# Attention with a learned distance bias, and a routed mixture of experts: the 64-row last tile of a batch regrouped from four units into two, with the planner's choices for the bias blocks and its ranks changed

## The chip, the cores and the metric

The kernel runs on one core of a Trainium2 chip. The metric is device time in microseconds (us) of one execution, the median of three runs: 261.92 us before the change (261.89 to 262.06).

## What is computed

Two batches of 8 heads, 576 positions and head size 64 go through attention; its rows, 1152 tokens of 512, go through a top-1 mixture of 8 experts with 288 places each. All arrays are float32.

```python
scores = scale * np.matmul(q, k.transpose(0, 1, 3, 2))
psi_rel = np.log1p(np.abs(rel))                    # rel = i - j
psi_i = np.log1p(np.maximum(pos[:, None], 1.0))
h = np.maximum((psi_rel / psi_i)[..., None] @ w1 + b1, 0.0)   # 32 hidden
scores = scores + (h @ w2).transpose(2, 0, 1)[None]           # a bias for each head, i, j
attn = softmax(scores)
x = np.matmul(attn, v)                             # to [1152, 512]
# each token: the expert with the largest gate logit, the first 288 tokens of an expert in order
out = gate * (relu(x_e @ w1_e) @ w2_e)             # 0 for tokens without a place
```

## The kernel before, in words

**Attention.** A batch's 576 rows are five tiles of rows: t = 0 to 3 hold 128 rows, t = 4 holds 64. The work runs over `units` (L507): the tiles of batch 0 in the order 4, 3, 2, 1, 0, then of batch 1 in the order 0 to 4, and in each tile four pairs of heads, 40 units in all. For a unit the planner has these tasks:

- S (`scores`, L181): the scores. In a 128-row tile, the two heads of a pair lie on the two halves of the array's rows, so four matmuls of 64 x 128 weights and 288 columns fill two PSUM buffers `s` (L195). In the 64-row tile, q is stored with zeros between the heads, so that two matmuls of the full array (L203) give both heads of the pair in one buffer: one head in partitions 0 to 63, the other in 64 to 127.
- L (`least`, L206): adds the bias and takes the row minimum of the negated scores (one VectorE instruction of 128 x 576 at L212; two for a unit of a 128-row tile, one for one of the 64-row tile). X (`expo`): the exponential on ScalarE (L219), with row sums.
- R and T (`transp_rem`, `transp`): transposes of the exponentials on TensorE, the last 64 positions (L266 in the 64-row tile) and the others (L241 there; `flips` at L227 in the other tiles); C: copies out of PSUM by ScalarE or VectorE (L250, L252, L273).
- V (`attn_v`, L275): values times transposed exponentials, the two heads on the two halves of the array's columns (L289; in the 64-row tile L292 with 64 columns, and L295 on two quadrants).

R, T, C and V of a unit follow two units (`LAG`) behind its S.

**The bias.** It depends on the rows alone, so both batches use it. 36 blocks of 16 rows each (`blocks`: tile 4's four blocks first, then those of tiles 3, 2, 1, 0) are made in this way: H, four instructions of the hidden layer (`hidden`, each a quarter c of the rows; GpSimd L122, ScalarE L124, VectorE L126); M, eight TensorE instructions on four column strips of the array (L141); E, a scaling out of PSUM by VectorE or ScalarE (L154, L156); D, a store to DRAM (L162). B loads a tile's bias back, skewed (L175, L178), once all its blocks are stored.

**Experts.** Routing constants and picks are small VectorE work. Expert weights come by 512 KB loads issued by GpSimd (L686), are split into two parts (L668, L670, L673) and used in three matmuls for each product (L723, L764, L792, L828). Most of the buffers for the second and third expert's weights take the place of attention's, so a task `late` lets them begin behind the last V.

**The order of work.** Every task has engines to choose from with a cost on each, tasks it comes after, buffers it takes, and a rank. `place_tasks` (L951) simulates the engines' queues with those costs and issues the tasks in the order it finds: of the tasks that can start within 0.3 us of the earliest, the one of least rank, on the engine that ends it first. `shift` adds a number to the rank of a kind of task. Before the planner starts, constants, the first K tiles and the first q are loaded. The order of each engine's queue is thus fixed when the program is built. The sync queue (SP) issues all stores and loads but the expert weights, indirect gathers and scatters, in order; a wait there holds all that stands behind.

## Time and profile before

| | |
|---|---|
| median of three runs | 261.92 us |
| the profiled execution | 260.9 us, its span 259.1 us |
| TensorE matmuls busy | 238.8 us, 92% of the span |
| VectorE, ScalarE, GpSimd busy | 194.0, 180.9, 106.9 us |
| moved by DMA | 58.63 MB, 226 GB/s over the span |

A busy TensorE is one with a matmul in flight; matmuls overlap, so their costs are best read from one start to the next. In the traces PE is TensorE, PEld its weight loads, DVE VectorE, ACT ScalarE, POOL GpSimd, SP the sync engine; a "q" behind a name is the engine's instruction queue. Tiles have the program's names: `s`, `tt`, `pt`, `av` are PSUM buffers, `ed` the scores and exponentials, `bt` the loaded bias, `bd` the bias in DRAM, `bo` a block of it ahead of its store, `hid` the hidden layer, `vt` the values.

### The profile page before, as it was taken

The numbers are of one execution on the slowest core, as the hardware profiler recorded it, in microseconds if no ns is written. First come the engines' busy times: TensorE is split into PE (matmuls) and PEld (weight loads), VectorE is DVE, ScalarE is ACT, GpSimd is POOL, SyncE is SP. The second block draws the span as 40 slices with busy tenths as digits, with TensorE's granted clock in tenths as the row PEclk, the third lists the DMA queues.
The fourth block names the chain that finished last, engine by engine and source line by source line (L and its number), as shares of the span: only waits on it lengthen the run. The fifth ranks groups of instructions, "written<-read, shape, count | busy, mean of one in ns | idle before, by whom it ended". The sixth has DMA issues, their size and how long they took to land.

```text
span 259.1 us, 7407 instructions
## 1 busy us (share of the span) xinstructions
PE 238.8 (92%) x2820; PEld 186.0 (72%) x2820; DVE 194.0 (75%) x551; ACT 180.9 (70%) x405; POOL 106.9 (41%) x112
## 2 busy tenths in 40 slices
PE   1997988999999999999999999999999999999950
PEld 0642544767755888888888877878898999999830
DVE  3898978999785756568989989588955799985200
ACT  4998998999998878787888778745202498832410
POOL 2999999999970200000123222001105948000410
PEclk9999999999999999999999999999999999999995
DMA  5589999989897862398689999800223799700210
GB/s 162 189 314 214 394 367 336 337 250 395 263 367 299 283 238 63 108 325 299 184 274 375 293 249 357 320 0 3 81 83 122 273 401 411 307 0 4 61 48 3
DMA packets 26620, 58.63 MB, mean 226 GB/s; under 512 B 3573, under 2 KB 4341, under 8 KB 26577
## 3 DMA queue, kind: packets, MB, share of 16 engines
q1 hardware_dynamic: 22224, 43.02, 49.6%
q0 software_dynamic: 4352, 15.06, 16.0%
q8 instruction: 24, 0.39, 0.6%
q14 instruction: 20, 0.16, 0.2%
HBM read 41.36 MB, written 16.99 MB: 225 GB/s over the span
## 4 chain that ended last, share of the span: by engine, by line
PE 69%; DMA 11%; issue 6%; DVE 5%; ACT 3%; POOL 2%; POOLq 0%; SPq 0%; DVEq 0%
PE s L195 11%; PE av L289 11%; PE tt L227 5%; PE s L764 5%; PE pt L723 5%; DMA bd<-bo 5%; PE tt L141 3%; PE pt L141 3%; DMA raw<-in_w_dram 3%; PE tt L764 3%; PE pt L764 3%; DMA bt<-bd 2%; PE s L203 2%; PE s L141 2%; PE tt L723 2%
## 5 line engine op out<-in xcount | busy, mean ns | idle before, releaser
L122 POOL TENSOR_SCALAR hid<-c_u,nbv 128x384 f32<-128x384 f32 (+17 forms) x48 | 68.7, 1447 | 2.2 <-PE tt L141 1.3
L212 DVE CUSTOM_DVE_ANT_0 ed<-s,bt 128x576 f32<-128x576 f32 x72 | 51.9, 754 | 18.4 <-PE s L227 12.0
L219 ACT ACTIVATE ed<-ed,mn 128x576 f32<-128x576 f32 x72 | 55.9, 785 | 2.1 <-DVE kept L584 1.3
L250 ACT COPY at<-tt 128x512 f32<-128x512 f32 x68 | 37.6, 590 | 17.9 <-PE tt L227 14.0
L195 PE MATMUL s<-kraw,q 64*128 64x288 f32 x256 | 40.8, 426 | 0.9 <-DVE rt L273 0.8
L289 PE MATMUL av<-at,vt 128*64 128x128 f32 x512 | 35.1, 279 | 0.0
L289 PEld LDWEIGHTS av<-at,vt 128*64 128x64 f32 x512 | 27.4, 136 | 6.0 <-issue 4.9
L195 PEld LDWEIGHTS s<-kraw,q 64*128 64x128 f32 x256 | 24.1, 186 | 9.5 <-issue 3.7
L126 DVE TENSOR_SCALAR hid<-c_u,c_v 128x464 f32<-128x464 f32 (+17 forms) x52 | 29.2, 609 | 0.1
L673 DVE TENSOR_TENSOR wl<-raw,wh 128x1024 fp32r<-128x1024 f32 x24 | 28.8, 1214 | 0.3 <-ACT wh L668 0.3
L124 ACT ACTIVATE hid<-c_u,c_v 128x448 f32<-128x448 f32 (+16 forms) x44 | 26.9, 668 | 2.9 <-DVE c_v L528 2.9
L434 POOL TENSOR_SCALAR tokv<-s 128x5 bf16<-128x5 f32 (+2 forms) x3 | 0.6, 206 | 67.8 <-DVE s L428 51.9
L686 POOL DMA_DIRECT2D raw<-in_w_dram x24 | 13.3, 560 | 27.7 <-DVE wl L673 15.7
L227 PE MATMUL tt<-c_ident,ed 64*128 64x64 f32 x512 | 22.6, 223 | 0.0
L227 PEld LDWEIGHTS tt<-c_ident,ed 64*128 64x128 f32 x512 | 19.6, 139 | 2.5 <-issue 0.5
L141 PE MATMUL pt<-hid,c_w2bd 128*32 128x496 f32 (+11 forms) x144 | 17.4, 513 | 1.8 <-ACT bo L156 1.0
L141 PE MATMUL tt<-hid,c_w2bd 128*32 128x512 f32 (+11 forms) x160 | 18.0, 471 | 0.1
L668 ACT CAST wh<-raw 128x1024 fp32r<-128x1024 f32 x16 | 16.8, 1049 | 0.5 <-DMA raw<-in_w_dram 0.4
L156 ACT ACTIVATE bo<-pt,corr,c_rv 128x192 f32<-128x192 f32 (+25 forms) x26 | 14.1, 595 | 0.9 <-PE pt L141 0.6
L493 POOL DMA_INDIRECT xe<-xd,sli x7 | 8.7, 1248 | 14.5 <-DVE hl L730 8.2
L219 ACT ACTIVATION_READ_ACCUMULATOR ed<-ed,mn 128x1 f32 x72 | 14.7, 204 | 0.0
L748 POOL DMA_INDIRECT out_dram<-y,sli x7 | 8.2, 1164 | 15.3 <-ACT sh L842 8.9
(272 smaller groups left out, 511.9 us busy)
## 6 DMA issues: line engine op xcount, KB each, us to landing
bt<-bd SPq DMA_DIRECT2D x28, 576.0 KB, 5.7
raw<-in_w_dram POOLq DMA_DIRECT2D x24, 512.0 KB, 7.0
bd<-bo SPq DMA_DIRECT2D x36, 295.5 KB, 5.8
vt<-in_v_dram SPq DMA_DIRECT2D x8, 320.0 KB, 5.2
kraw<-in_k_dram SPq DMA_DIRECT2D x8, 288.0 KB, 4.3
bt<-bd SPq DMA_DIRECT2D x8, 288.0 KB, 6.5
out_dram<-y SPq DMA_DIRECT2D x3, 768.0 KB, 12.5
q<-in_q_dram SPq DMA_DIRECT2D x8, 256.0 KB, 5.8
```

The lines of the kernel that those rows point to most:

```text
L122: nc.gpsimd.tensor_scalar(hid[:, :m], wu[:, :m], nbv[:, w:w + 1], None, op0=ALU.max)
L124: nc.scalar.activation(hid[:, :m], wu[:, :m], AF.Relu, bias=bvw[:, w:w + 1])
L126: nc.vector.tensor_scalar(hid[:, :m], wu[:, :m], bvw[:, w:w + 1], 0.0, op0=ALU.add, op1=ALU.max)
L141: nc.tensor.matmul(ps[32 * c:32 * c + 32, lo:hi], lhsT=w2bd, rhs=hids[n, c][:, lo:hi], start=True, stop=True, tile_position=(0, 32 * c))
L195: nc.tensor.matmul(ps[i][:, r, :HALF], lhsT=q[p, hp], rhs=k[p, r * HALF:(r + 1) * HALF], start=True, stop=True, tile_position=(64 * i, 0))
L212: nc.vector.tensor_tensor_reduce(out=ed.rearrange("p (r j) -> p r j", r=2), in0=ps[:, :, :HALF], in1=bias.rearrange("p (r j) -> p r j", r= ...
L219: nc.scalar.activation(ed, ed, AF.Exp, scale=-1.0, bias=mns.pop((n, i)), accum_out=total)
L227: nc.tensor.transpose(out[r][:w], ed[p, o:o + w], ident[p, p], tile_position=(64 * r, 0))
L250: nc.scalar.copy(o, v)
L289: nc.tensor.matmul(av[p, hp], lhsT=vt[:, j, i], rhs=at[:, 4 * i + j] if j < 4 else rt, start=(j == 0), stop=(j == 4), tile_position=(0, r))
L673: (nc.vector if eng == "d" else nc.gpsimd).tensor_tensor(lo, raw, hi.bitcast(F32), op=ALU.subtract)
L764: nc.tensor.matmul(py[:, :cap], lhsT=w, rhs=hx, start=(f + i == 0), stop=(f == 7 and i == 2))
```

## The change

- The 64-row tile of a batch has two units of two pairs of heads each instead of four units of one pair, 36 units in all. q of this tile is stored without zeros. Scores are eight matmuls of 64 x 64 weights on the four quadrants of the array (row half: head of the pair, column half: the pair), into two `s` buffers. L, X, R, T and C are then those of a 128-row tile, and V is two pairs' worth of matmuls with 64 columns; both pairs' K must be there for a unit, so the second K tile is loaded earlier.
- H of the first eight blocks may go to VectorE or ScalarE only (GpSimd was a choice for c = 3 of blocks 0 to 3, the only one for c = 3 and one of three for c = 2 of the others); for the other blocks c = 2 goes to ScalarE or GpSimd. Costs of H are new numbers, with another one for VectorE while GpSimd is at work.
- Loads of V of batch 0, the gate weights and the routing constants wait for no task; `v` has 8 buffers (4 before), `q` has 2 (3 before).
- The `shift` table has new numbers throughout, and new kinds: S, L, X, R, T, V and C by pairs of tiles, H, M, E, D by tile.

The core of the diff:

```diff
-    qp = keep.enter_context(tc.tile_pool(name="qp", bufs=3))
-    vp = keep.enter_context(tc.tile_pool(name="vp", bufs=4))
+    qp = keep.enter_context(tc.tile_pool(name="qp", bufs=2))
+    vp = keep.enter_context(tc.tile_pool(name="vp", bufs=8))
...
     def scores(n):
 
         b, t, hp = units[n]
-        if t < 4:
-            sc = [big.tile([128, 2, 512], F32, name="s") for _ in range(2)]
+        ps = [big.tile([128, 2, 512], F32, name="s") for _ in range(2)]
...
-        q, k = qs[b, t], raws[b, hp]
-        if t < 4:
-            ps = sc
-            for r in range(2):
+        q = qs[b, t]
+        for r in range(2):
+            for c, u in enumerate(pairs(n)):
+                o, w = (0, 128) if t < 4 else (64 * c, 64)
                 for i in range(2):
                     p = slice(64 * i, 64 * i + 64)
-                    nc.tensor.matmul(ps[i][:, r, :HALF], lhsT=q[p, hp], rhs=k[p, r * HALF:(r + 1) * HALF],
-                                     start=True, stop=True, tile_position=(64 * i, 0))
...
-        ps = big.tile([128, 2, 512], F32, name="s")
-        free[n] = [ps[:, r] for r in range(2)]
-        for r in range(2):
-            nc.tensor.matmul(ps[:, r, :HALF], lhsT=q[:, hp], rhs=k[:, r * HALF:(r + 1) * HALF], start=True, stop=True)
-        sx[n] = [(ps, ed[:, 0], sums_t[b, t][:, hp:hp + 1])]
+                    nc.tensor.matmul(ps[i][o:o + w, r, :HALF], lhsT=q[p, u, :w], rhs=raws[b, u][p, r * HALF:(r + 1) * HALF],
+                                     start=True, stop=True, tile_position=(64 * i, o))
+        free[n] = [z[:, 1] for z in ps]
...
     def attn_v(n):
...
+        for c, u in enumerate(pairs(n)):
+            o, w = (0, 128) if t < 4 else (64 * c, 64)
+            for j in range(5):
+                for i in range(2):
+                    r = 64 * i
+                    nc.tensor.matmul(av[r:r + 64, u, :w], lhsT=vs[b, u][:, j, i],
+                                     rhs=(at[:, 4 * i + j] if j < 4 else rt)[:, o:o + w],
                                      start=(j == 0), stop=(j == 4), tile_position=(0, r))
...
-    units = [(0, t, hp) for t in (4, 3, 2, 1, 0) for hp in range(4)] + \
-            [(1, t, hp) for t in (0, 1, 2, 3, 4) for hp in range(4)]
+    units = [(b, t, z) for b, t in order for z in range(4 if t < 4 else 2)]
...
     dma_q(*order[0])
+    dma_k(0, 1)
     ident = load_const("ident", [128, 128])
-    for hp in range(1, 4):
+    for hp in range(2, 4):
         dma_k(0, hp)
...
+        def cost(us, e, at):
+
+            return us["dp"] if e == "d" and "dp" in us and free_at["p"] > at else us[e]
...
-            engines = "p" if c == 3 and n >= 4 else "dap" if c == 2 and n >= 4 or c == 3 else "da"
-            task(("H", n, c), engines, {"d": 0.12 + m * 1.1e-3, "a": 0.2 + m * 0.83e-3, "p": m * 3.4e-3},
+            engines = "da" if n < 8 else ("da", "da", "ap", "p")[c]
+            task(("H", n, c), engines, {"d": 0.2 + m * 0.52e-3, "dp": 0.37 + m * 0.62e-3, "a": 0.2 + m * 0.83e-3, "p": 0.36 + m * 2.35e-3},
...
-            task(("VL", b, hp), "s", 0.45, (lambda b=b, hp=hp: dma_v(b, hp)), after=[slot(17) if b else slot(hp - 1) or then("B", 0, 4, 1)],
-                 rank=20.0 * b + hp - 1, takes=[("v", users)], kb=273)
-    task("wg", "s", 0.45, lambda: nc.sync.dma_start(out=wgt, in_=ins["wg"]), after=[slot(1)], rank=4.0, kb=32)
-    task("route", "s", 2.7, route_const, after=[slot(6)], rank=12.0, kb=300)
+            task(("VL", b, hp), "s", 0.45, (lambda b=b, hp=hp: dma_v(b, hp)), after=[slot(p1 - 3) if b else None],
+                 rank=p1 * b + hp - 1, takes=[("v", users)], kb=273)
+    task("wg", "s", 0.45, lambda: nc.sync.dma_start(out=wgt, in_=ins["wg"]), rank=4.0, kb=32)
+    task("route", "s", 2.7, route_const, rank=12.0, kb=300)
...
-        task(("V", n), "e", 1.15 if full else 0.79, (lambda n=n: attn_v(n)),
+        task(("V", n), "e", 1.15 if full else 1.6, (lambda n=n: attn_v(n)),
...
-    qr = np.zeros((B, 2, D, 4, 2, 64), f4)
-    for r in range(2):
-        qr[:, r, :, :, r] = qT[:, :, r::2, 512:]
+    qr = qT[:, :, :, 512:].reshape(B, D, 4, 2, 64).transpose(0, 3, 1, 2, 4)
```

## Rows read from the trace of the kernel before

**Rows 1.** The chain that ended last, by engine (the page's part 4).

```profile
PE 69%; DMA 11%; issue 6%; DVE 5%; ACT 3%; POOL 2%; POOLq 0%; SPq 0%; DVEq 0%
```

**Rows 2.** By stretch: us, busy PE, PEld, DVE, ACT, POOL, clock, DMA share, GB/s.

```profile
10.00:80.00 70.00, 66.07 (x813) 37.79 (x809) 61.87 (x147) 65.84 (x144) 65.24 (x49) 1.00 0.93 318
20.00:42.00 22.00, 18.71 (x199) 8.71 (x193) 18.95 (x45) 20.68 (x46) 22.00 (x18) 1.00 1.03 332
42.00:85.00 43.00, 42.36 (x589) 27.15 (x586) 35.54 (x93) 39.63 (x90) 33.81 (x26) 1.00 0.91 319
85.00:160.00 75.00, 73.90 (x1096) 61.37 (x1096) 60.00 (x195) 60.33 (x155) 11.59 (x17) 1.00 0.77 253
160.00:250.00 90.00, 89.40 (x826) 81.22 (x821) 64.59 (x192) 44.14 (x91) 24.08 (x37) 1.00 0.43 157
```

**Rows 3.** The chain in order of time, 20 to 42 us: start, us, what.

```profile
22.46 6.53 DMA bd<-bo
...
34.54 5.27 DMA bt<-bd
```

**Rows 4.** Timeline of the sync queue, 0 to 30 us: start, us, engine, line, what.

```profile
4.62 1.38 SPq L84 DMA_DIRECT2D kraw<-in_k_dram  x3
10.27 5.75 SPq L162 DMA_DIRECT2D bd<-bo  x6
16.07 0.44 SPq L105 DMA_DIRECT2D vt<-in_v_dram  x1
16.70 4.07 SPq L178 DMA_DIRECT2D bt<-bd  x4
...
28.21 0.33 SPq L105 DMA_DIRECT2D vt<-in_v_dram  x1
```

**Rows 5.** Timeline of TensorE, 150 to 260 us.

```profile
157.40 1.24 PE L195 MATMUL s<-kraw,q 64*128 64x288 f32 x8
158.48 0.22 PE L227 MATMUL s<-c_ident,ed 64*128 64x64 f32 x2
...
159.13 0.43 PE L324 MATMUL pt<-xT,wgt 128*32 128x128 f32 x8
...
167.82 1.13 PE L203 MATMUL s<-kraw,q 128*128 128x288 f32 x4
168.88 0.33 PE L266 MATMUL s<-c_ident,ed 64*64 64x64 f32 x4
169.14 0.46 PE L241 MATMUL tt<-c_ident,ed 64*128 64x64 f32 x8
169.53 0.21 PE L415 MATMUL pt<-acc,ones 128*128 128x24 bf16 x2
...
182.56 0.69 PE L292 MATMUL av<-at,vt 128*64 128x64 f32 x16
183.18 0.33 PE L295 MATMUL av<-rt,vt 64*64 64x64 f32 x4
183.44 0.33 PE L336 MATMUL s<-c_ident,lT 128*128 128x128 f32 x1
```

**Rows 6.** Timeline of TensorE, 0 to 45 us.

```profile
28.71 0.72 PE L141 MATMUL tt<-hid,c_w2bd 128*32 128x304 f32 x8
29.36 0.69 PE L292 MATMUL av<-at,vt 128*64 128x64 f32 x16
```

**Rows 7.** VectorE's groups by form, 5 to 22 us: count, busy us, mean ns, idle.

```profile
L126 DVE TENSOR_SCALAR hid<-c_u,c_v 128x576 f32<-128x576 f32 x1 | 0.5, 514 | 0.0
```

**Rows 8.** VectorE's groups by form, 50 to 72 us.

```profile
L126 DVE TENSOR_SCALAR hid<-c_u,c_v 128x576 f32<-128x576 f32 x2 | 1.8, 960 | 0.0
```

**Rows 9.** GpSimd's instructions of line 122 alone, 5.5 to 21 us.

```profile
5.50:21.00 15.50, 14.93 (x10) 1.00 0.72 242
```

**Rows 10.** VectorE's instructions of line 126 alone, 5.5 to 21 us.

```profile
5.50:21.00 15.50, 11.48 (x19) 1.00 0.72 242
```

**Rows 11.** ScalarE's hidden-layer group of the page's part 5.

```profile
L124 ACT ACTIVATE hid<-c_u,c_v 128x448 f32<-128x448 f32 (+16 forms) x44 | 26.9, 668 | 2.9 <-DVE c_v L528 2.9
```

More of the change, by code (lines that the diff above doesn't have):

```diff
@@ L105, in dma_v @@
         nc.sync.dma_start(out=vs[b, hp], in_=ins["v"][b, hp])
-    blocks = [32, 33, 34, 35] + [8 * t + i for t in (3, 2, 1, 0) for i in range(8)]
+    order = [(0, 4), (0, 3), (0, 2), (0, 1), (0, 0), (1, 0), (1, 1), (1, 2), (1, 3), (1, 4)]
+    first = list(dict.fromkeys(t for _, t in order))
+    blocks = [8 * t + i for t in first for i in range(8 if t < 4 else 4)]
     bps = {}
@@ L169, in skewed @@
         return bass.AP(tensor=v.tensor, offset=v.offset, ap=ap)
+    loads = [0]
+    for u, w in zip(order, order[1:]):
+        loads.append(loads[-1] + (u[1] != w[1]))
     def dma_bias(b, t, g):
@@ L505, in fetch, with pairs @@
             fetch_rows(z, x, nt, a)
-    units = [(0, t, hp) for t in (4, 3, 2, 1, 0) for hp in range(4)] + \
-            [(1, t, hp) for t in (0, 1, 2, 3, 4) for hp in range(4)]
+    units = [(b, t, z) for b, t in order for z in range(4 if t < 4 else 2)]
     NU = len(units)
     LAG = 2
-    order = [units[4 * i][:2] for i in range(10)]
+    def pairs(n):
+        _, t, z = units[n]
+        return (z,) if t < 4 else (2 * z, 2 * z + 1)
     man = ExitStack()
@@ L1049 @@
+    task("route", "s", 2.7, route_const, rank=12.0, kb=300)
     for n, (b, t, hp) in enumerate(units):
-        n0 = unit0[b, t]
+        p = pos[n]
         full = t < 4
         rem = [("R", n - LAG)] if n >= LAG else []
-        src = [("K", b, hp)] if b else []
-        src += [("Q", b, t)] if n0 else [("M", 3)]
-        task(("S", n), "e", 1.09 if full else 1.07, (lambda n=n: scores(n)), after=src + [slot(n - 1)], rank=n - 0.5,
-             takes=[("s", [("L", n, i)] + ([("C", n - LAG, 2)] if rem else [])) for i in two(n)]
+        src = [("K", b, u) for u in pairs(n)] if b else []
+        src += [("Q", b, t)] if (b, t) != order[0] else [("M", 3)]
+        task(("S", n), "e", 1.09, (lambda n=n: scores(n)), after=src + [("S", n - 1) if n else None], rank=p - 0.5,
+             takes=[("s", [("L", n, i)] + ([("C", n - LAG, 2)] if rem else [])) for i in range(2)]
@@ L1063 @@
-        bias = ("B", 0 if (b, t) == (1, 0) else b, t, hp if full else hp // 2)
-        for i in two(n):
-            task(("L", n, i), "d", 0.69, (lambda n=n, i=i: least(n, i)), after=[("S", n), bias] + rem, rank=n + 0.1 + 0.01 * i,
+        task(("R", n), "e", 0.07, (lambda n=n: transp_rem(n)), after=[("X", n, i) for i in range(2)] + ([] if last else [("S", n + LAG)]),
+             rank=p + LAG - 0.6, takes=[("s", [("C", n, 2)])] if last else [])
+        task(("T", n), "e", 0.56, (lambda n=n: transp(n)), after=[("R", n)], rank=p + LAG - 0.55,
+             takes=[("tt", [("C", n, i) for i in range(2)])])
@@ L1066 @@
+        bias = ("B", *order[loads.index(loads[order.index((b, t))])], hp)
+        for i in range(2):
+            task(("L", n, i), "d", 0.69, (lambda n=n, i=i: least(n, i)), after=[("S", n), bias] + rem, rank=p + 0.1 + 0.01 * i,
                  takes=[("mn", [("X", n, i)])])
-            task(("X", n, i), "a", 0.78, (lambda n=n, i=i: expo(n, i)), after=[("L", n, i)], rank=n + 0.1 + 0.01 * i)
+            task(("X", n, i), "a", 0.78, (lambda n=n, i=i: expo(n, i)), after=[("L", n, i)], rank=p + 0.1 + 0.01 * i)
@@ L1072 @@
-        task(("V", n), "e", 1.15 if full else 0.79, (lambda n=n: attn_v(n)),
-             after=[("C", n, i) for i in two(n)] + [("C", n, 2), ("VL", b, hp), ("V", n - 1) if n else None],
-             rank=n + LAG + 0.7, takes=[("av", [("A", b, t)])] if hp == 0 else [])
+             after=[("R", n)] + ([("L", n + LAG, i) for i in range(2)] if not last else []), rank=p + LAG + 0.3, takes=[("rt", [("V", n)])])
+        task(("V", n), "e", 1.15 if full else 1.6, (lambda n=n: attn_v(n)),
+             after=[("C", n, i) for i in range(3)] + [("VL", b, u) for u in pairs(n)] + [("V", n - 1) if n else None],
+             rank=p + LAG + 0.7, takes=[("av", [("A", b, t)])] if hp == 0 else [])
```

148 lines of the change are left out of this document (58 added, 90 removed), and 20 rows, old and new, of the table shift.

## The prediction, made before the changed kernel ran

> **What bounds the kernel now.** I read the chain that ended last first. By engine, 69% of the span lies on TensorE, 11% on DMA, 6% in issue and 5% on VectorE [rows 1]: one engine is the path for most of the span, and where it isn't, a transfer is. Next I read the busy time by stretch, to see where that is so [rows 2]. From 42 to 85 us TensorE is busy for 42.36 of 43 us, from 85 to 160 for 73.90 of 75, from 160 to 250 for 89.40 of 90: packed, with 2.3 us of gaps in 208. From 20 to 42 it is busy for 18.71 of 22, and there the DMA share is 1.03. So there are two regimes. Ahead of 42 us the bias supply decides: the chain from 22.46 to 39.8 us is nothing but bias stores, from one that takes 6.53, and a bias load of 5.27 from 34.54 on [rows 3], and then comes the first score reduction of the second tile. Behind 42 us every microsecond taken from TensorE's own list moves the end, as long as what feeds it keeps up. In the stretch from 10 to 80 us the feeders are close to full too: ScalarE 65.84, VectorE 61.87, GpSimd 65.24 of 70 us [rows 2]. The granted clock is 1.00 in all five stretches, the upper level (2.4 GHz), so no term below changes with it.
>
> **The last tile's matmuls.** Prices are start to start on TensorE, so that they hold weight loads and drains [rows 5]. A unit of the 64-row tile now: scores 1.06 us (167.82 to 168.88), remainder 0.26, transposes 0.39, values 0.88 (182.56 to 183.44): 2.59, four times, 10.36 us a tile. Two units take their place. Their remainder and transposes are a full unit's, 0.65 (158.48 to 159.13). The values become 40 instructions of 64 columns; 16 such take 0.62 now (182.56 to 183.18), so 1.55. The scores become 16 instructions of 288 columns on 64x64 quadrants, and no row of before has four quadrants at work. One such instruction alone costs 0.265 (1.06 / 4). Bounds: all four at once, 4 x 0.265 = 1.06; only two at once, as the row halves of a full unit run now (eight in 157.40 to 158.48, 1.08), 2.16. The nearest row is the bias matmul, four column strips: eight instructions of 304 columns in 0.65 us [rows 6], where one alone would be 0.28, so 3.4 at once. I take that: 16 x 0.265 / 3.4 = 1.25. A new unit is 0.65 + 1.55 + 1.25 = 3.45, two are 6.90, and a tile saves **3.5 us** (3.8 with four at once, 1.6 with two).
>
> There is one reason to doubt it. In rows 6 the weight loads of four strips that share all rows of the array don't keep the strips apart. The Trainium skill, TensorE: Matmul & The Clock Gate, Part 3 (Packing small matmuls), says the opposite: a weight load overlaps matmuls in flight only when its row group differs. By it the two column halves of a row half would follow one another, scores would cost 2.16, and the tile would save 1.6. The trace disagrees for column strips (0.65 against 8 x 0.28 = 2.24); no run here yet shows quadrants.
>
> The second batch's such tile runs between 160.9 and 198 us, in the packed stretch, where the matmuls of the first expert fill every wait: the whole 3.5 counts. The first batch's runs from 14.5 to 49 us, mostly where transfers decide. Of it only the last remainder, transposes and two values stand behind 42 us, and the new second unit's own share is as long, so I count nothing there by itself. On VectorE and ScalarE the reductions, exponentials and 512-element copies keep their number (four units of one, two units of two); four small copies a tile go away, under 1 us on engines that are not the path behind 85 us.
>
> **Loads at the start.** The four V loads of batch 0 stood in the sync queue from 16.07 to 28.21, between the bias stores and ahead of bias loads [rows 4]; now nothing holds them back, and the queue is idle from 6.0 to 10.27 us. Each is 128 x 640 x 4 = 328 KB, and at the 332 GB/s of the stretch from 20 to 42 us [rows 2] takes 0.99 us, 4.0 for the four, in just the stretch where the DMA share is over 1. What they are moved past: they, one q load, the gate weights and the seven routing constants now go ahead of the first bias store, some 13 issues at 0.43, 5.6 us against 4.3 idle, so the first stores may slip by about 1.3. Behind them waits the first bias load (16.70), and behind it VectorE's first reduction. That slip is paid from the gain only if it is still there at 34.5, when the second tile's bias is loaded. Ends: nothing, and 4.0 us. The gain can't be taken whole, because ScalarE has only 4.2 us left in 70 [rows 2] to do its work sooner. I take 2, the middle, because the transfer is the chain there [rows 3] but the engines behind it are nearly full.
>
> **Bias blocks.** For the first eight blocks GpSimd is no longer a choice; behind them the third quarter is ScalarE's or GpSimd's, no longer VectorE's. GpSimd did 10 such instructions up to 21 us, 14.93 us of its time [rows 9]. At ScalarE's 0.67 each [rows 11] they are 6.7 us on two engines, 3.3 us later. Against it: the same VectorE instruction took 0.51 us beside a gap of GpSimd [rows 7] and 0.96 beside a busy one [rows 8], and VectorE ran 19 of them in that stretch [rows 10], so at 0.2 each (less than half of that difference, most being shorter rows) it gets 3.8 back. Net nothing, ends 1 us sooner and 3 later. The cover is that VectorE's speed-up; if it isn't there, the first stores are late by up to 3 us, which eats the loads' gain. The ranks, new throughout, have no price in a row. What an order can win in the packed stretches is their 2.3 us of gaps; what it can lose is about the same. Zero, ends plus and minus 1.5.
>
> **Sum.** 3.5 + 2.0 = 5.5 off the profiled execution of 260.9 us (a span of 259.1 and 1.8 around it): 255.4. That execution lies 1.0 below the median of the runs shown, 261.92, so **256.4**. A measurement can tell about 0.2%, 0.5 us, from no change.
>
> **The rivals.** (a) *Quadrants run as pairs.* Speaks for it: row halves run two at once, no row shows more than strips. The tile saves 1.6, the start 2.0: 258.3. (b) *The whole of both tiles counts.* If the bias comes 4.0 sooner and the freed 3.5 us of the first tile let matmuls of later blocks start ahead of 42 us, 7.0 + 4.0 = 11 come off: 250.9. Against it: ScalarE's 4.2 idle us from 10 to 80. (c) *The freed time is handed back.* The chain at the end turns to the weights: from 200 us on the splits and loads of the second and third expert wait for the last V of attention, and if the new order ends attention no sooner, TensorE merely does expert matmuls earlier and waits later. Then only the start counts or nothing: 260 to 262. Against it: no gaps in 90 us now. (d) *Slower: the bias supply falls behind.* Place: blocks 8 to 35, from about 20 to 75 us. VectorE may not take the third quarter any more, GpSimd is already busy 65 of 70 us, and the 10 instructions it did early must go to ScalarE or VectorE. If ScalarE gets all 10 and keeps its waits, the stream of tiles is 10 x 0.67 = 6.7 us later, and 6.7 - 3.5 = 3.2 slower: 265.1. It decides from 3.5 us of lateness on. Against it: VectorE has 8.1 us idle in the same 70. (e) That the change doesn't do what it says, four units still standing, can't be: the diff makes two units of the tile and no other path is left.
>
> **How the numbers follow.** Forecast 0.54; (a) 0.12; (b) 0.14; (c) 0.11, a third of it within the 0.5 us of no change; (d) 0.09. The forecast's own ends, quadrants at 3.8 and loads at 4.0 with ranks at -1.5, or loads at 0 with ranks at +1.5, are 252.6 and 259.9. The range from 251.5 to 260.4 holds the forecast, (a), half of (b) and a part of (c); outside are the rest of (b), the flat part of (c) and (d), about 0.2. Faster: 0.54 + 0.12 + 0.14 + 0.06 = 0.86; same 0.05; slower 0.09.
>
> **What would show it.** Scores of the 64-row tile: 16 instructions start to start in 1.06 to 1.3 us is right, about 2.1 is (a). Values in 40 instructions at 1.55. The stretch of the second such tile should hold about 3.5 us less TensorE work, and the last V should come sooner by the whole saving. At the start V loads ahead of 11 us, the first reduction of the second tile ahead of 39.8 by 1 to 4 us. VectorE's hidden-layer instructions before the eighth block at about 0.5 us. I'm wrong if gaps appear on TensorE behind 42 us, if the second tile's first reduction comes later than 39.8, or if the last V comes no sooner.

## The result, and the profile after

The changed kernel takes 265.77 us (265.36 to 267.12) beside 261.90 for the kernel before on the same chip: a ratio of 1.0148, 95% interval 1.0118 to 1.0178. It is slower by 3.9 us where 5.5 less were forecast. The profiled execution is 265.38 us with a span of 263.6, 4.5 more than before. Ratios, here and below, are taken over the fast executions alone and medians over all, so a ratio need not be the quotient of two medians.

TensorE's own work did shrink, from 238.8 to 236.4 us busy. What it does not work grew more, from 20.3 to 27.2 us of the span. The busy time by stretch of the changed kernel, columns as in [rows 2]:

```profile
10.00:80.00 70.00, 62.16 (x761) 31.72 (x757) 60.00 (x146) 63.21 (x136) 62.01 (x44) 0.98 0.86 287
20.00:42.00 22.00, 16.25 (x134) 5.36 (x130) 14.80 (x34) 16.59 (x35) 20.44 (x17) 0.92 0.89 275
42.00:85.00 43.00, 42.52 (x619) 26.64 (x616) 39.53 (x101) 41.28 (x95) 32.58 (x24) 1.00 0.84 291
85.00:160.00 75.00, 72.99 (x1051) 59.26 (x1047) 58.64 (x186) 57.22 (x145) 10.19 (x16) 1.00 0.79 258
160.00:250.00 90.00, 87.82 (x894) 80.17 (x892) 70.39 (x205) 42.69 (x93) 22.41 (x35) 1.00 0.45 161
```

Against [rows 2], TensorE lost 3.91 us of 10 to 80, all before 42, and got gaps behind 85 us: 2.0 instead of 1.1, then 2.2 instead of 0.6. The sync queue of the changed kernel shows the first loss, to be read against [rows 4]:

```profile
6.48 0.43 SPq L100 DMA_DIRECT2D q<-in_q_dram  x1
6.95 2.45 SPq L105 DMA_DIRECT2D vt<-in_v_dram  x4
9.44 0.65 SPq L1042 DMA_DIRECT2D wgt<-in_wg_dram  x1
10.13 0.65 SPq L533 DMA_DIRECT2D ltri<-in_ltri_dram  x1
...
12.29 0.33 SPq L533 DMA_DIRECT2D tokv<-in_tokv_dram  x1
13.08 0.33 SPq L533 DMA_DIRECT2D iota<-in_iota_dram  x1
13.92 0.33 SPq L533 DMA_DIRECT2D etab<-in_etab_dram  x1
14.82 0.33 SPq L533 DMA_DIRECT2D acc<-in_acc_dram  x1
15.27 2.95 SPq L164 DMA_DIRECT2D bd<-bo  x5
...
20.42 2.58 SPq L184 DMA_DIRECT2D bt<-bd  x4
```

The first bias store is issued at 15.27 instead of 10.27 us, the first bias load at 20.42 instead of 16.70. What waits for it, in the timelines of VectorE and of TensorE:

```profile
27.34 0.76 DVE L211 CUSTOM_DVE_ANT_0 ed<-s,bt 128x576 f32<-128x576 f32 x1 [3.77 <-DMA bt<-bd]
```

```profile
28.16 2.53 PE L202 MATMUL s<-kraw,q 64*64 64x288 f32 x16 [3.13 <-DVE mn L211]
```

The first score minimum starts at 27.34 instead of 23.64 us, TensorE stands for 3.13 us, and its next scores run partly at the lower clock (1.2 GHz; the granted clock is 0.71 from 28 to 31 us, 0.92 over 20 to 42): 2.53 us for what takes 1.13 at the upper level (2.4 GHz). The last tile itself is as it was meant to be; TensorE's timeline in the second batch:

```profile
165.90 1.20 PE L202 MATMUL s<-kraw,q 64*64 64x288 f32 x16
167.03 0.27 PE L226 MATMUL s<-c_ident,ed 64*128 64x64 f32 x2
...
185.43 0.69 PE L269 MATMUL av<-at,vt 128*64 128x64 f32 x16
185.94 0.29 PE L269 MATMUL av<-rt,vt 128*64 128x64 f32 x4
186.06 0.64 PE L269 MATMUL av<-at,vt 128*64 128x64 f32 x16
186.53 0.29 PE L269 MATMUL av<-rt,vt 128*64 128x64 f32 x4
186.74 0.40 PE L702 MATMUL pt<-xh,wh 128*128 128x288 f32 x1
```

Scores of a unit take 1.13 us (165.90 to 167.03), its values 1.31 (185.43 to 186.74). The last values end at 189.9 instead of 198.1 us, and yet the last matmul comes 4.6 us later. The chain that ended last has TensorE on 42% instead of 69% [rows 1]:

```profile
PE 42%; issue 14%; DVE 12%; DMA 7%; ACT 4%; POOL 2%; POOLq 1%; ACTq 0%
```

### The profile page after: what moved, and what is told of

It is laid out like the page before. It is cut to its first block, busy times and chain, and to the rows that moved or that the text cites. A ratio compares the mean times of both kernels' runs of the same rounds, so it can differ in the third digit from the quotient of the medians.

```text
span 263.6 us, 7394 instructions
## 1 busy us (share of the span) xinstructions
PE 236.4 (90%) x2828; PEld 179.5 (68%) x2828; DVE 198.9 (75%) x560; ACT 175.2 (66%) x393; POOL 99.7 (38%) x107
## 4 chain that ended last, share of the span: by engine, by line
PE 42%; issue 14%; DVE 12%; DMA 7%; ACT 4%; POOL 2%; POOLq 1%; ACTq 0%
PE av L269 11%; PE s L202 11%; DMA raw<-in_w_dram 6%; PE tt L226 6%; PE pt L143 3%; PE pt L702 3%; PE tt L143 2%; DVE wl L652 2%; PE pt L319 2%; DVE ed L211 2%; DVE hl L709 1%; ACT bo L158 1%; POOL out_dram L727 1%; DMA xd<-x 1%; DVE match L438 1%
## 5 line engine op out<-in xcount | busy, mean ns | idle before, releaser
L124 POOL TENSOR_SCALAR hid<-c_u,nbv 128x304 f32<-128x304 f32 (+17 forms) x43 | 61.8, 1452 | 10.3 <-PE tt L143 5.1
L202 PE MATMUL s<-kraw,q 64*128 64x288 f32 (+1 forms) x320 | 47.4, 433 | 4.0 <-DVE mn L211 3.1
L269 PE MATMUL av<-at,vt 128*64 128x128 f32 (+1 forms) x640 | 40.6, 268 | 1.1 <-ACT ed L218 1.0
L202 PEld LDWEIGHTS s<-kraw,q 64*128 64x128 f32 (+1 forms) x320 | 27.4, 178 | 16.4 <-DVE mn L211 5.2
L241 ACT COPY at<-tt 128x512 f32<-128x512 f32 x56 | 30.8, 587 | 8.5 <-PE tt L226 7.9
L652 DVE TENSOR_TENSOR wl<-raw,wh 128x1024 fp32r<-128x1024 f32 x24 | 28.8, 1219 | 3.3 <-ACT wh L647 3.2
L128 DVE TENSOR_SCALAR hid<-c_u,c_v 128x400 f32<-128x400 f32 (+16 forms) x59 | 29.4, 556 | 0.0
L126 ACT ACTIVATE hid<-c_u,c_v 128x576 f32<-128x576 f32 (+17 forms) x42 | 26.5, 689 | 3.0 <-DVE c_v L507 3.0
L143 PE MATMUL pt<-hid,c_w2bd 128*32 128x400 f32 (+12 forms) x160 | 20.7, 532 | 3.4 <-ACT bo L158 2.3
L269 PE MATMUL av<-rt,vt 128*64 128x128 f32 (+1 forms) x160 | 15.0, 262 | 0.0
L158 ACT ACTIVATE bo<-pt,corr,c_rv 128x128 f32<-128x128 f32 (+21 forms) x22 | 12.0, 595 | 2.9 <-PE pt L143 2.8
```

The source lines that it names most:

```text
L124: nc.gpsimd.tensor_scalar(hid[:, :m], wu[:, :m], nbv[:, w:w + 1], None, op0=ALU.max)
L126: nc.scalar.activation(hid[:, :m], wu[:, :m], AF.Relu, bias=bvw[:, w:w + 1])
L128: nc.vector.tensor_scalar(hid[:, :m], wu[:, :m], bvw[:, w:w + 1], 0.0, op0=ALU.add, op1=ALU.max)
L143: nc.tensor.matmul(ps[32 * c:32 * c + 32, lo:hi], lhsT=w2bd, rhs=hids[n, c][:, lo:hi], start=True, stop=True, tile_position=(0, 32 * c))
L202: nc.tensor.matmul(ps[i][o:o + w, r, :HALF], lhsT=q[p, u, :w], rhs=raws[b, u][p, r * HALF:(r + 1) * HALF], start=True, stop=True, tile_pos ...
L241: nc.scalar.copy(o, v)
```

## The experiments

Three theories of the loss stood. 1: the loads that wait for nothing stand ahead of the first bias store. 2: the engines chosen for the hidden layer are the wrong ones. 3: the refitted ranks lose the middle and the tail. A fourth came with the runs, F below: the time saved in the last tile is worth nothing where it is saved. All runs, each ratio against the kernel before on the same chip (its medians there: 261.4 to 263.0); "store" and "minima" are the first bias store and the first score minimum of the first and second tile, "idle" is TensorE not busy from 10 to 42 and from 160 to 230 us, all from the profiled execution:

| run | median us | ratio (95%) | store | minima | idle |
|---|---|---|---|---|---|
| before | 261.9 | 1 | 10.27 | 23.64, 39.83 | 3.29, 0.11 |
| changed | 265.77 | 1.0148 (1.0118 to 1.0178) | 15.27 | 27.34, 40.90 | 7.36, 2.18 |
| changed, again | 265.03 | 1.0141 (1.0099 to 1.0183) | 16.76 | 28.23, 42.61 | 7.84, 1.92 |
| all loads back | 265.33 | 1.0115 (1.0076 to 1.0155) | 10.74 | 24.73, 41.67 | 7.61, 3.47 |
| constants back | 264.17 | 1.0062 (1.0020 to 1.0105) | 10.75 | 24.65, 40.12 | 4.71, 2.46 |
| V back | 263.20 | 1.0023 (0.9992 to 1.0053) | 11.80 | 23.67, 39.60 | 5.93, 3.14 |
| V between | 264.15 | 1.0142 (1.0078 to 1.0206) | 10.78 | 26.10, 41.45 | 6.81, 1.84 |
| two V in front | 263.35 | 1.0055 (1.0017 to 1.0092) | 10.63 | 24.34, 39.89 | 4.79, 2.12 |
| two V, GpSimd helps | 266.83 | 1.0147 (1.0079 to 1.0216) | 10.68 | 28.04, 41.39 | 7.03, 3.55 |
| old engines | 267.72 | 1.0205 (1.0139 to 1.0271) | 16.05 | 27.96, 43.38 | 4.79, 1.69 |
| old ranks | 268.42 | 1.0265 (1.0217 to 1.0312) | 15.97 | 27.27, 40.73 | 6.69, 5.38 |
| tile alone, both batches | 267.11 | 1.0138 (1.0048 to 1.0229) | 11.47 | 26.65, 42.87 | 3.48, 3.77 |
| tile alone, second batch | 263.11 | 1.0045 (1.0008 to 1.0082) | 10.27 | 23.25, 39.92 | 3.22, 3.77 |
| weights first | 268.26 | 1.0242 (1.0162 to 1.0322) | 10.76 | 25.23, 39.36 | 4.39, 4.66 |
| tile alone, x sooner | 263.82 | 1.0054 (1.0018 to 1.0089) | 10.34 | 22.89, 39.63 | 2.45, 4.10 |
| two V, x sooner | 262.75 | 1.0028 (0.9992 to 1.0063) | 10.64 | 24.12, 39.90 | 4.77, 3.32 |

The profiled execution is not always a typical one: it took 267.94 us with all loads back, 265.05 with V back and 268.37 with GpSimd's help, each time the slowest of its run.

**The control** is the changed kernel as it stands.

> The changed kernel once more, as the control for the three that run beside it: 265.4 to 266.5 us, ratio to the kernel before 1.012 to 1.018.

Its ratio came out as expected, its time 0.4 us below the lower end.

**The loads.** In five runs the planner's order stays and only the named tasks are issued later in SP's queue, behind an anchor task. The edit as two V in front has it; the first three runs do the same in another form:

```diff
-            fn(*([e] if len(engines) > 1 else []), *(p for p, (pools, _) in zip(chosen, takes) if len(pools) > 1))
+            calls.append((name, fn, [e] if len(engines) > 1 else [], [p for p, (pools, _) in zip(chosen, takes) if len(pools) > 1]))
+        back = {("B", 0, 4, 1): (("VL", 0, 2), ("VL", 0, 3), "wg", "route")}
...
+            c[1](*c[2], *c[3])
+            for d in back.get(c[0], ()):
+                moved_back[d][1](*moved_back[d][2], *moved_back[d][3])
```

All loads back:

> Against the changed kernel (265.8 us), with every rank, engine and order left alone: the four V loads, the gate weights and the seven routing constants are issued behind the last tile's bias loads instead of ahead of the first bias store. Theory 1 (these loads block SP's queue): first bias store issued at 10.3 to 11 us instead of 15.27, first score-minimum on VectorE at 23.6 to 24.5 instead of 27.34, no stretch of half clock before 40 us, and the gain of about 3 us stays to the end: 262.5 to 263.5. Theory 2 (the engines chosen for the hidden layer cost it): first store early all the same, but the bias blocks bound the first 85 us and the end stays within 0.7 us of 265.8. Theory 3 (the refitted ranks lose the time in the middle and in the tail): the start gains 3 us and the waits at 123 us (routing of group 0 ahead of the minima), at 143 us (weights split on ScalarE) and in the tail take it back: 265 to 266.

Constants back (`"wg", "route"` alone):

> As the run with all loads moved, but only the gate weights and the seven routing constants go behind the bias loads; the four V loads stay at the head of SP's queue. If the eight small issues are what holds the queue (5.8 us of 15.27, from 9.44), the first store comes at about 9.5 to 10.6 us and the first minimum at about 24: the time is that of the run with all loads moved, within 0.5 us. If the V loads' bytes are what the late first minimum comes from (2.6 MB beside the stores), the first minimum stays at 25.5 or later and the time within 1 us of 265.8.

V back (the four `VL` alone):

> Only the four V loads go behind the bias loads; gate weights and routing constants stay ahead of the first store. Theory 1, with the slow constants as the culprit: first store at 12.5 to 13 us (the V loads gave 2.5 us), first minimum at about 25.3, the time at about 264.5. With the V loads as the culprit: first minimum at 24 and the time as in the run with all loads moved.

V between (`("D", 3)` as V's anchor, the constants behind the bias loads):

> The changed kernel with the order of every other engine left alone: V loads behind the fourth bias store and ahead of the last tile's bias loads, gate weights and routing constants behind those loads. In the two runs where V went behind the bias loads the first stores were early, but TensorE stood idle for 4 to 5 us at 30 to 42 us; where V stayed in front, the first minimum was 1 us late. If the place of V is what is left of the start's loss: first store at 10.7, first minimum at 23.7 to 25, TensorE's idle time of 30 to 42 us at 1.5 to 2.3, and 261.5 to 263. If the start's loss is the bias supply (hidden layer on GpSimd, evictions on ScalarE) and not the queue: 263 to 264.5, with TensorE idle or waiting inside the bias products all the same.

Two V in front (`VL` 2 and 3, `wg` and `route` back):

> The changed kernel, order of all else left alone: of the four V loads only the two that the first unit's values need stay ahead of the bias stores; the other two, the gate weights and the routing constants go behind the last tile's bias loads. If bytes and issues ahead of the bias loads cost the first minimum and a late V costs TensorE at 30 to 42 us, both shrink: first store 10.7, first minimum at 23.7 to 24.5, TensorE idle at 30 to 42 us under 2.5, and 261.5 to 263 against 265.0 for the changed kernel. If the start's loss is the bias supply, as the run with V between stores and bias loads suggested (264.2): 264 to 265.

The first store follows theory 1: 10.6 to 10.8 us, 11.8 with the constants still ahead. What each of the two groups costs is less plain. V back alone takes away most of the slowdown: from 1.0141 to 1.0023, 1.2% or 3.1 us, with the intervals apart. Constants back gains 0.8%, V between stores and bias loads nothing: there the bias loads are issued at 18.13 us, as in V back (18.32), but the first minimum comes 8.0 us behind that instead of 5.4, with V's bytes just ahead. V back was to be worse than constants back by my guess that the slow constants are the culprit; it came out at least as well (263.20 us where 264.5 was expected), so that guess falls. I had also taken TensorE's gaps at 30 to 42 us in the runs with V behind the bias loads for waits on V. The rows name something else; TensorE's timeline of V back:

```profile
31.76 0.74 PE L143 MATMUL pt<-hid,c_w2bd 128*32 128x320 f32 x8 [1.28 <-ACT bo L158]
...
40.67 2.03 PE L202 MATMUL s<-kraw,q 64*128 64x288 f32 x7 [1.55 <-ACT rt L256]
```

The waits are for the bias blocks' evictions (`bo`, their scaling out of PSUM), and for a copy that stands behind a minimum of the second tile. That minimum waits for its bias load; with two V in front, VectorE's waits from 29 to 43 us:

```profile
DVE ed L211 <- DMA bt<-bd: 2.5, 1, 2.5
```

The best of these five runs reach a second tile's minimum at 39.6 to 39.9 us, the kernel before's 39.83, and none is more than 0.3 us ahead of it. By these waits the bias blocks through DRAM set that point with either tile. Two V in front lead the changed kernel by 0.86% (1.0141 to 1.0055, 2.2 us), the two intervals apart. All loads back has its first minimum 2.6 us sooner than the changed kernel's 27.34 and next to nothing at the end, which by itself looks like theory 3; why both groups together win less than either is not settled.

**The engines.** GpSimd takes 4 of the 32 hidden instructions of the first eight blocks again, the rest as with two V in front:

```diff
+            if c[0][0] == "H" and 4 <= c[0][1] < 8 and c[0][2] == 3:
+                c = (c[0], c[1], ["p"], c[3])
```

> The run with two V loads in front, and the fourth hidden group of the second four blocks on GpSimd as it was before (4 of the 32 instructions that the change gives to VectorE and ScalarE). Theory 2 (VectorE and ScalarE, full from 10 to 20 us, set when the first bias blocks are stored, while GpSimd has 1.3 of 10 us at work): first minimum or the second tile's 0.5 to 1.5 us sooner, the kernel 0.5 to 1.5 us faster than the run with two V loads. Against it (GpSimd slows VectorE beside it, 0.39 us an instruction alone and 0.67 beside, and its own instruction takes 1.5): same or slower by up to 1 us.

```profile
PE tt L143 <- POOL hid L124: 3.2, 1, 3.2
```

That is TensorE's longest wait from 10 to 42 us there: the four instructions arrive late, the first minimum is at 28.04, and the median is 3.5 us higher than with two V in front (1.0147 beside 1.0055, with intervals that just overlap). GpSimd had little room for them: there it was at work for 7.8 of the 10 us from 10 to 20, not 1.3. Then the engines and costs of before, planned anew with the new ranks:

```diff
-            engines = "da" if n < 8 else ("da", "da", "ap", "p")[c]
-            task(("H", n, c), engines, {"d": 0.2 + m * 0.52e-3, "dp": 0.37 + m * 0.62e-3, "a": 0.2 + m * 0.83e-3, "p": 0.36 + m * 2.35e-3},
+            engines = "p" if c == 3 and n >= 4 else "dap" if c == 2 and n >= 4 or c == 3 else "da"
+            task(("H", n, c), engines, {"d": 0.12 + m * 1.1e-3, "a": 0.2 + m * 0.83e-3, "p": m * 3.4e-3},
```

> The changed kernel with the hidden layer's engines and their costs as before (GpSimd from the fifth block on, sometimes on two groups of four), planned anew with the new ranks. If the engines are the loss: first minimum no earlier (the loads still stand ahead), but TensorE's time in the bias products falls from 37 to 35.5 us and the kernel takes 263 or less. If GpSimd slows it, as the change supposes: 266 to 268.

Not faster either (1.0205 beside 1.0141, with intervals that overlap), and TensorE's bias products take 41.0 us from start to start, more than the changed kernel's 37.2, where 35.5 was expected. So neither run bears theory 2 out. They don't settle it: the old engines ran with ranks fitted to the new ones, and TensorE's waits from 10 to 42 us do name ScalarE's evictions, in the changed kernel

```profile
PE pt L143 <- ACT bo L158: 2.3, 3, 1.3
PE tt L143 <- ACT bo L158: 0.7, 2, 0.5
```

and in the kernel before

```profile
PE pt L141 <- ACT bo L156: 1.0, 2, 0.6
```

With two V in front these waits are 2.4 us, 1.4 more than before, and TensorE's idle time of 10 to 42 us is 1.5 more than before. No run had engines and ranks fitted together.

**The ranks.** The table and the kinds of before in the changed kernel:

> The changed kernel with the table of rank shifts (and its kinds) of before, planned anew; tile, loads and engines stay changed. If the refitted ranks are what loses the middle and the tail (theory 3): TensorE's idle time behind 85 us falls from 4.2 to about 2 and the kernel takes 263 or less. If the ranks were fitted to just this tile, these loads and these engines, the old ones fit worse: 266 to 270.

3.4 us slower than the changed kernel. Theory 3 falls as I had put it: with this tile, these loads and these engines the new ranks are better than the old ones.

**The tile alone.** Loads, engines and ranks of before, both batches' last tiles in two units, planned anew:

> The kernel before with the last tile as two units alone: conditions of the loads, the hidden layer's engines with their costs, and the ranks are those of before; planned anew from these. If the tile is worth what the trace of the changed kernel shows (scores -2.98 us of TensorE, values -1.60, transposes -0.85 over two batches): 261.9 - 3.5 to 5 = 257 to 258.5, and loss and surplus of the change lie in loads, engines and ranks. If the old ranks, never fitted to this tile, leave the freed time unused (what I gave as the chain turning to the weights behind the last values): 260 to 262. If quadrants themselves cost it (bank hand-over, waits of the next unit): above 262.

It took 267.11 us (1.0138), the range that I had given for the quadrants themselves costing it. That reading is not shown: the whole order changed with it, the first store went out at 11.47 us and the second tile's first minimum came at 42.87, long before the second batch's tile runs.

The second batch's tile alone, where the plan up to it hardly moves:

```diff
+                for c, u in enumerate(pairs(n)):
...
+                        o, w, x = (0, 128, 0) if t < 4 else (64 * c, 64, 64 * i)
...
-            [(1, t, hp) for t in (0, 1, 2, 3, 4) for hp in range(4)]
+            [(1, t, hp) for t in (0, 1, 2, 3) for hp in range(4)] + [(1, 4, z) for z in range(2)]
```

> The kernel before, in which only the second batch's last tile is cut into two units of quadrants and pairs; the first batch's last tile, the loads, the engines and the ranks stay as they were. Theory T (the tile is worth what TensorE's rows say, in a stretch where TensorE has no idle time): the minima before it stand where they stood (last full unit's at about 162.3 us), the last values end some 3 to 4 us sooner than at 198.1, and the kernel takes 258 to 259. Theory F (nothing is won because what follows is not ready sooner: the routing of the last tokens, the weights' order): the last values end sooner, TensorE's idle time behind 200 us grows by the same 3 us, and the kernel takes 261 to 262.5.

This is the run that decides. The last tile's first minimum is at 163.2 us (162.3 before), its last values end at 188.3, and it is slower than before by 0.45%. TensorE by stretch:

```profile
160.00:200.00 40.00, 36.96 (x466) 31.33 (x466) 31.41 (x118) 17.99 (x47) 4.71 (x11) 1.00 0.32 109
200.00:205.00 5.00, 4.33 (x21) 4.32 (x22) 1.06 (x5) 0.40 (x1) 4.39 (x8) 0.67 0.69 226
```

Before, TensorE was busy for 39.89 us of 160 to 200. Here 3.04 us are idle, among them waits of 0.82, 0.40 and 1.21 us from 196.9 on, and right behind them the clock falls. TensorE's timeline there:

```profile
200.67 0.40 PE L786 MATMUL s<-hh,wl 128*128 128x288 f32 x1 [1.21 <-DVE wl L695]
200.91 0.29 PE L786 MATMUL s<-hh,wh 128*128 128x288 f32 x1
...
202.29 0.44 PE L786 MATMUL pt<-hh,wl 128*128 128x288 f32 x1
202.53 0.44 PE L786 MATMUL pt<-hh,wh 128*128 128x288 f32 x1
...
205.27 0.29 PE L786 MATMUL pt<-hh,wh 128*128 128x288 f32 x1
205.40 0.30 PE L786 MATMUL pt<-hl,wh 128*128 128x288 f32 x1
```

The same matmul starts every 0.24 us at the lower level and every 0.13 at the upper. In this run theory F holds: the saved time became idle time, and in the profiled execution (263.99 us) some 1.9 us of slow matmuls came on top (the second layer's start to start, 28.8 us instead of 27.0). The clock does not fall so far in each of its executions: five with a mean of 0.986 or 0.987 took 260.9 to 263.5 us, five at 0.977 to 0.982 took 263.0 to 266.0. One thing stays open: the order behind the tile was planned anew with ranks that had been fitted to the longer tile, and another order might leave less idle.

**What TensorE's time is worth there.** First three of five key blocks of that tile's values left out of the kernel before:

> The kernel before, order and plan left alone, with 12 of the 20 value products of each unit of the second batch's last tile left out (3 of 5 key blocks), so that TensorE has some 2.5 to 3 us less to do between 171 and 198 us and nothing else changes. Theory T (TensorE bounds there): 258.5 to 259.5. Theory F (a chain through VectorE, the x store, the gathers and the weights sets what follows, and TensorE is only packed beside it): within 0.6 us of the kernel before, and TensorE's idle time of 0.1 us at 160 to 200 us grows by 2 us or more.

293.43 us in all, which says nothing: without them other tokens go to other experts, and there is more for the experts to do. Up to 212 us, though, TensorE's list is in the order of the kernel before. Each of the four units has 0.35 us less from start to start (0.53 instead of 0.88), 1.4 in all. A product ahead of them and one behind them, in the kernel before:

```profile
181.98 0.29 PE L723 MATMUL pt<-xh,wl 128*128 128x288 f32 x1
...
198.42 0.29 PE L764 MATMUL tt<-hl,wh 128*128 128x288 f32 x1
```

and here:

```profile
182.40 0.29 PE L723 MATMUL pt<-xh,wl 128*128 128x288 f32 x1
...
193.71 0.40 PE L723 MATMUL pt<-xh,wh 128*128 128x288 f32 x1 [0.26 <-DVE x L375]
...
198.10 0.30 PE L764 MATMUL tt<-hl,wh 128*128 128x288 f32 x1
```

From 0.42 us behind, the list came to 0.32 ahead: with the order kept, some 0.74 of the 1.4 us were won up to there, and part of the rest is a wait for VectorE. What that would be worth at the end can't be read from this run.

The other way round leaves the output alone: values computed twice, in the last tile of the second batch, of the first, and in a tile of 128 rows.

```diff
-        for j in range(5):
+        for j in [*range(5)] * (2 if (b, t) == (1, 4) else 1):
```

> The kernel before with the 20 value products of each unit of the second batch's last tile issued twice, the second time over the first (the sum is started anew), everything else left alone: 4 us more of TensorE between 171 and 198 us, from the price the tile's values have in the trace (16 in 0.69, 4 in 0.33 us). Theory F (behind the last full tile a chain of small steps sets the time, and TensorE's time there is worth little): +0 to +1.5 us. Theory T (TensorE bounds there): +3.5 to +4.5 us. If it costs the full 4 while taking 3.4 us away won nothing, TensorE and the chain are level in the kernel before: both bind at once, and only work taken from both is won.

> The same for the first batch's last tile: 4 us more of TensorE between 29 and 42 us. If the bias supply sets the pace there (hidden layer, evictions, stores, loads), as the changed kernel's tile suggested, whose saving there went into slower bias products (25.2 us instead of 21.6 for the same 200): +0 to +1.5 us. If TensorE does: +3.5 to +4.5.

> The same for a tile of 128 rows in the packed stretch (the second batch's second tile, 20 products of 1.24 us in each of 4 units, 5 us more): the control for the other two. TensorE has about 1 us of idle time in 75 there: +4 to +5 us by both theories.

| run | median us | ratio (95%) | TensorE busy us | span us |
|---|---|---|---|---|
| last tile | 265.53 | 1.0122 (1.0050 to 1.0193) | 242.8 | 263.4 |
| first tile | 265.47 | 1.0105 (0.9996 to 1.0215) | 242.1 | 262.9 |
| 128 rows | 265.94 | 1.0132 (1.0054 to 1.0210) | 244.3 | 264.6 |

In the profiled executions each span grows by about what TensorE has more to do (4.0 and 4.3; 3.3 and 3.8; 5.5 and 5.5 us). The ratios alone are too wide to part 1.5 from 4 us, in the first tile above all; it is the spans that do, one execution each. For the last tile the third reading fits them: more work costs its price, and less, in the run with the tile alone, won nothing. By these, TensorE and something beside it were level.

**What stands beside it.** Two candidates were tried. The second expert's weight loads, issued only behind the gathers at 201 us, ahead of them:

```diff
+        back = {("B", 0, 4, 1): (("VL", 0, 2), ("VL", 0, 3), "wg", "route"), ("FM", 0, 7): tuple(("WL", 1, c) for c in (3, 4, 5, 6, 7))}
```

> The run with two V loads in front, and in GpSimd's queue five of the eight weight loads of the second expert moved ahead of the three gathers, for which they waited until 201 us though their buffers were free at 188.5 and nothing else held them. If the weights behind the gathers are what is late in the tail: the second expert's products and the end come 1 to 2.5 us sooner, 261 to 262.3, at or under the kernel before. If the chain is the x store and the gathers themselves (third gather at 222 us, TensorE idle 0.8 to 1.9 us for it): within 0.7 us of that run (263.3).

GpSimd's and TensorE's timelines of that run:

```profile
190.38 3.50 POOL L665 DMA_DIRECT2D raw<-in_w_dram  x6 [2.14 <-DVE slt L462]
200.08 1.04 POOL L468 DMA_INDIRECT xe<-xd,sli  x1 [6.20 <-DVE s L367]
```

```profile
203.76 0.28 PE L682 MATMUL pt<-c_ident,xe 96*128 96x96 f32 x1 [1.18 <-DMA xe<-xd,sli]
205.28 0.42 PE L682 MATMUL pt<-c_ident,xe 96*128 96x96 f32 x1 [1.25 <-DMA xe<-xd,sli]
```

Its ratio is 1.0242 where two V in front had 1.0055: the gathers come 3.3 us later than there (196.81) and TensorE waits for them. So moving the weights alone wins nothing; since the gathers slipped with it, this run can't clear them. For them speaks that in the changed kernel, with two V in front and with the tile alone no wait of TensorE from 160 to 252 us names a weight load. The x store that the gathers wait for was moved next, in the run with the tile alone and, behind another anchor, in the one with two V in front:

```diff
+        back = {('MT', 1, 7): (("BM", 1, 2), ("BX", 1, 2), ("BD", 1, 2))}
```

> The run with the second batch's last tile alone in two units, and one thing moved: turning back, scaling and storing x of the second batch's third tile (its logits were done at 162 us, its x stood behind the seventh first-layer product and was stored only at 194.87 us) goes ahead of the fifth first-layer product, the order of all else left alone. If that x store and the three gathers of the second expert's rows behind it (197.8 us, their indices ready at 190.3) are what TensorE runs out of work for, when the tile takes 3.4 us less: gathers from 190.5 to 191.5 us, the second expert's weight loads from 195 instead of 201.5, TensorE's idle time at 160 to 200 us from 3.7 to under 2.5 and no half clock at 200 to 205: 259 to 261.5 against 263.1, at or under the kernel before. If the first expert's own steps (its split weights on VectorE, one bank of accumulators) leave TensorE idle: the gathers come early and the time stays within 0.7 us of 263.1.

> The same x moved in the run with two V loads in front (the changed kernel with its other loads put back): x store at 192.72 and gathers at 196.5 us there, indices ready at 191. Theory gathers: gathers from 191 to 192, TensorE's idle time of 200 to 230 us (1.3) falls, 261.5 to 262.5 against 263.3. Theory first expert: within 0.5 us of 263.3.

GpSimd with the tile alone and x sooner:

```profile
191.33 1.05 POOL L505 DMA_INDIRECT xe<-xd,sli  x1 [0.31 <-DVE slt L501]
...
193.98 1.23 POOL L505 DMA_INDIRECT xe<-xd,sli  x1 [0.30 <-issue]
200.35 2.32 POOL L708 DMA_DIRECT2D raw<-in_w_dram  x4 [5.14 <-DVE slt L499]
```

The gathers come 6.4 us sooner, at 191.33, the weight loads hardly (200.35 instead of 201.46), and TensorE is idle from 160 to 200 no less (3.93 us). With two V in front they come 3.9 us sooner (192.87). The medians of both stay where they were, so the gathers alone are not it either. The profiled execution of the tile alone with x sooner is also one in which the clock held (1.00 from 160 to 230 us): its span is 260.0 us beside 259.1 before, so the idle time by itself eats the saving. TensorE's waits from 160 to 206 us there name VectorE almost throughout:

```profile
PE s L786 <- DVE slt L498: 1.2, 1, 1.2
PE tt L355 <- DVE lg L379: 0.9, 1, 0.9
PE pt L745 <- DVE x L387: 0.8, 1, 0.8
PE pt L355 <- DVE hl L752: 0.8, 1, 0.8
PE pt L492 <- ACT slots L487: 0.4, 1, 0.4
```

These are the first expert's own small steps (hidden parts, and with x not moved its split weights) and the last tokens' routing, one after another on VectorE. No run took them away, so that they are the level partner is argued from the rows and not shown. V back (1.0023) and two V with x sooner (1.0028) come nearest to the kernel before and are not told apart from it; no run beat it.

## Why the prediction was wrong

- **Last tile, TensorE's price: right.** A unit's scores take 1.13 us (1.25 estimated, bounds 1.06 and 2.16), its values 1.31 (1.55). With the second batch's tile alone, TensorE's attention work from start to start falls by 3.7 us (3.5 forecast). Rival (a) is out. The rule weighed there (the Trainium skill, TensorE: Matmul & The Clock Gate, Part 3, Packing small matmuls), as I read it, gives 2.16 us for the 16 quadrant matmuls; they took 1.13, so the trace disagrees for quadrants as it did for strips.
- **"The whole 3.5 counts": the first step that failed.** I read packed from 0.6 us of gaps in 90 and took it that nothing else was level. With the tile alone TensorE had 3.7 us less to do in attention and was idle for 2.9 us more from 160 to 200; the kernel took 1.2 us more instead of 3.5 less, an error of 4.7. That is rival (c), handed back, but not at the place I gave: I put it at the second expert's weights, and TensorE's waits name VectorE's steps. I also wrote there "no gaps in 90 us now" as the argument against; gaps were the wrong thing to ask for.
- **"Loads at the start", 2.0 gained: the second step that failed.** It cost 2 to 3 us (constants back gains 2.1, two V in front 2.2, V back 3.1, though all loads back only 0.7), an error of 4 to 5. I saw the slip, priced 13 issues at 0.43 as 5.6 us against 4.3 idle, and got 1.3. They took 8.8 (6.48 to 15.27), and the slip was 5.0. The gate weights and the seven constants alone took 5.8 of it, the last ones 0.8 to 0.9 us apart; that is only in part V's doing, since in V back they took 4.9. The cover was about as assumed: with two V in front the first store goes out at 10.63, 4.1 us behind 6.48. And the gain had no place. I took the bias transfer from 34.54 for movable by V's bytes; wherever V went, the second tile's minimum came at 39.4 us at the earliest, 0.5 ahead of the kernel before.
- **First batch's tile, counted as nothing: about right, for a reason I did not give.** With two V in front, TensorE has the same 200 or so bias products done by 39.9 us, but in 25.2 us from start to start instead of some 22. The eight matmuls of one of its blocks and of a block of the same width before:

```profile
38.09 1.85 PE L143 MATMUL tt<-hid,c_w2bd 128*32 128x448 f32 x8
```

```profile
39.07 0.96 PE L141 MATMUL pt<-hid,c_w2bd 128*32 128x448 f32 x8 [0.86 <-ACT at L250]
```

  The first is from constants back; its strips start one by one from 38.09 to 39.41 us, so the group waits inside. And one part went the wrong way: no values of the first tile are done by 39.9 us, where before two units' were (1.75 us), because two units behind now means further behind. They fall in the packed stretch.
- **Bias blocks, net nothing: right in size as far as the runs show.** VectorE did 26 hidden instructions in 11.56 us up to 21 us, against 19 in 11.48 [rows 10], so the speed-up beside a quieter GpSimd (9.99 us of it instead of 14.93 [rows 9]) is there, 0.44 us each instead of 0.60, and giving GpSimd four instructions back cost 3.5 us by the medians. Rival (d) came nearest in time, 265.1. Its place, ScalarE on the blocks behind the eighth, holds a part of the loss, the 2 us more that TensorE waits for evictions up to 42 us; it does not run on from there to 75 us, where TensorE's gaps are no longer than before (0.48 instead of 0.64 us of 42 to 85).
- **Ranks, zero plus or minus 1.5: the bounds were too narrow.** Old ranks in the changed kernel cost 3.4 us; engines, loads and ranks are fitted to one another, and engines or ranks put back alone and planned anew were no better.
- **The sum.** Tile alone 0.45% and the loads by two V in front 0.86% are 1.31%, by V back 1.18% are 1.63%, against 1.41 to 1.48 measured. The runs are from different chips and each ratio is uncertain by about 0.4%, so the sum closes no better than that, and a part of the engines' is not excluded.

## What to carry to other kernels

A packed engine need not be the only bound: the planner here had filled every gap of TensorE, and by the rows other chains ran level with it unseen. Before counting saved time as won, ask what the engine would do in it, and which steps that work waits for; doubling the work shows the price upwards only, taking it away alone shows whether anything is won, in the order that is planned around it. A load that waits for nothing still takes its place in an in-order queue, and is priced by who stands behind it.

## What the runs showed of the hardware

- A row of small loads is not issued at the pace of one. The gate weights and the seven constants, at 0.43 us each, would be through in 3.4. From the first one's issue to that of what follows they took 4.85 us with no V ahead (V back, 6.95 to 11.80), 5.83 behind the four V loads (changed, 9.44 to 15.27) and 6.40 behind the bias loads and two V (two V in front, 21.50 to 27.90). The queue's waits name V's loads for 1.9 us in the changed kernel and a bias load for 1.3 with two V in front; what sets the pace where neither is ahead is not shown.
- A gap on TensorE can cost more than itself. In the profiled execution of the tile alone the clock fell behind the waits shown above, and the second layer took 1.9 us longer. In the 12 executions of tile alone, x sooner, the three with a mean granted clock of 0.985 to 0.987 took 261.8 to 262.9 us and the nine at 0.970 to 0.980 took 263.6 to 265.4, so some 2 us go with it; where the clock was low in the nine is not on record. With two V and x sooner the executions don't part in this way: 0.980 to 0.984 went with 262.1 to 263.9 us, 0.986 to 0.990 with 261.1 to 263.9.
